# Left-over tiles of an attention and mixture-of-experts kernel: the doubling of the gathered weights placed ahead of the expert loads, and the first table tied to the last batch's split weights

## The chip, the core and the metric

The kernel runs as one program on 1 core of a Trainium2 chip. The metric is the device time of one execution in microseconds; smaller is better. TensorE is called PE below, VectorE DVE, ScalarE ACT, GpSimd POOL and SyncE SP.

## The reference, cut to what matters

```python
B, N, C, A, E, F = 4, 11456, 128, 49, 8, 1024

a2k = softmax(scale * agents @ k.T)      # 49 agents attend over the N keys
agent_v = a2k @ v                        # 49 x 128 averages in each batch
x = softmax(scale * q @ agents.T) @ agent_v   # each token mixes the 49 averages

logits = x @ w_gate
e = argmax(logits)                       # one of 8 experts for each token
gate = softmax(logits)[e]
eom = sigmoid(x @ w_output_gate)[e]
out = gate * eom * (relu(x @ w1[e]) @ w2[e])
```

Inputs and outputs are float32. All tokens of a batch mix the same 49 averages, and most of a batch's tokens choose one expert. The rest choose others; they are the left-over ("left") tokens.

## The kernel before, in words

**Main stream.** Each batch is cut into 12 units of up to 1024 tokens, and these into 92 main tiles of up to 512 tokens. For a main tile every token is computed with the expert that most of its batch chose. The averages are folded into the expert's first matrix, so a main tile multiplies the softmax weights of its tokens (`x_ld`, transposed by DMA) with `w` to give `h`; ACT writes `hh` = relu(h) in float16, DVE the remainder `hl` = relu(h) - hh, and PE then forms `y` from `hh` and `hl` with the split second matrix `vv`. The weights of a batch are split into float16 halves in `first` and `second`; the last step of `second` stores the factor `i12` in `state[b]`.

**Left tiles.** The left tokens are computed in float32 in tiles of 128, with true experts, and their results are written over the main ones by an indirect DMA. `PHASES` has two entries: the left tokens of batches 0 and 1 fill up to 12 tiles (phase 0), those of batches 2 and 3 one tile (phase 1). For each phase `left_prepare` waits until the tokens of its batches are counted (`counted[0]`, which `q_tail` sets; 3 batches for phase 0, all 4 for phase 1), builds a table in `left_table` (tiles `pexc`, `ppi`, `cnt`, `tt`, much small DVE work), and then, for groups of 3, 3, 4 and 2 tiles, runs `left_index`, which works out the token numbers `ltu` and gathers with POOL indirect DMAs the tokens' softmax weights `ef` from DRAM into the tile `big` (`bigs` in phase 1). `got` notes for each tile the planned time `t` at which its gather is in.

`left_static` runs the left tiles in two ways, every other tile in each. Its helper `fronts` prepares one tile ahead: it waits until `t`, loads the two float32 matrices of the tile's expert (`left_load`, 512 KB each, SP queue, tiles `lw_ld`), waits until both are planned to be in, and calls `left_front`. This doubles the gathered weights (one DVE product, `big<-big,ltwo`: each weight times 0 or 1 for the two batches of the phase), transposes the 128 x 98 result on PE into the bank `let`, copies it with ACT, multiplies it with the averages (`lx`) and copies that (`lxs`). `left_back` then does the two expert products (`lh`, `ly`) and `left_store` the scatter. A tile of phase 1 does its `left_back` only when the main stream is through.

**What sets the order.** Nothing is reordered by a compiler. While the program is written, a planner (`Clock`) keeps a planned time for each engine, and coroutines (`spawn`, with a priority) offer their next instruction; it is emitted when the planner has its inputs ready and the engine free. Each engine then runs its own queue strictly in the emitted order and waits on semaphores where an input is late. `big` is in `clk.apart`, so the planner doesn't look at its readiness:

```python
            clk.apart.add(big.name)
```

The transposition may thus be emitted right behind the doubling that writes its input. A POOL gather is planned with 1100 ns on POOL and 2950 ns to land, and `got` adds 2000 ns in phase 0 (none in phase 1).

Of the kernel before, what the change touches and what calls it, by code (L numbers as in the profile page):

```python
# [18 lines left out]
B, N, C, A, E, F = 4, 11456, 128, 49, 8, 1024  # L19
# [249 lines left out]
def agent_attention_top1_moe(ctx, tc, qT, kT, v, aT, wg, wo, w1, w2, cst, sides, out):  # L269
    nc = tc.nc  # L270
    clk = Clock()
    ACT, DVE, POOL = Engine(clk, "ACT", nc.scalar), Engine(clk, "DVE", nc.vector), Engine(clk, "POOL", nc.gpsimd)
# [19 lines left out]
    def n_free():  # L292
        return sum(banks[k][0] for k in others)
# [4 lines left out]
    def first_free():  # L298
        return min((when_free(banks[k]), k) for k in others if banks[k][0])

    def bank(name, dt=F32, w=512, k=None):

        k = last[0] = first_free()[1] if k is None else k
        t = ps.tile([P, w], dt, tag=f"b{k}", bufs=1, name=name)
        banks[k][1] = t.name
        return t

    def hold(long=False):

        k = last[0]  # L310
        banks[k][0] = False
        if long:
            long_held.append((k, banks[k][1]))
        return k

    def release(k):
        banks[k][0] = True
# [11 lines left out]
    def wait_free(long=False):  # L329
        while True:  # L330
            long_held[:] = [x for x in long_held if not banks[x[0]][0] and banks[x[0]][1] == x[1]]

            keep = clk.started and (long or not (Y or resting[0]))
            if n_free() > keep and not (long and len(long_held) > 1) and first_free()[0] <= clk.now() + 50.0:
                return
            yield None
# [41 lines left out]
    for i in range(4):  # L378
        t = cp.tile([P, 8, P], F16, name=f"e16_{i}")
        e16s.append(t)  # L380
    avd = []
    for i in range(2):
        t = cp.tile([P, P + 32], F32, name=f"avd_{i}")
# [3 lines left out]
    for i in range(2):  # L387
        t = cp.tile([P, 2, 18], F16, name=f"gs_{i}")
# [5 lines left out]
    for i in range(2):  # L394
        t = cp.tile([P, E, NCOL], F32, name=f"oht_{i}")
# [59 lines left out]
    state = {}  # L455
# [9 lines left out]
    def spawn(g, prio=2):  # L465
        streams.append([prio, len(streams), g, None])
        streams.sort(key=lambda x: x[0])
# [92 lines left out]
    def scored(item):  # L560
        places[held.pop(item)][0] = True
# [614 lines left out]
    counted = [0]  # L1176
# [400 lines left out]
    def left_load(ph, ti, k, nm, at_=None):  # L1577
        b0, nb, _, _ = PHASES[ph]
        yield from SY.wait(ti)
        er = nc.values_load(ti[0:1, k, 0:1], engines=[SP], min_val=0, max_val=E - 1,  # L1580
                            skip_runtime_bounds_check_because=WHY)
        if at_ is None:
            w1t = wk.tile([P, F], F32, name=f"lw1{nm}", tag="w1t", bufs=2)
        else:
            w1t = yield from at_(f"lw1{nm}")
        yield from SY.q.dma_start(w1t, w1[bass.ds(er, 1)].rearrange("a p f -> p (a f)"))
        if at_ is None:
            w2t = wk.tile([P, F], F32, name=f"lw2{nm}", tag="w2t", bufs=2)
        else:
            w2t = yield from at_(f"lw2{nm}")  # L1590
        yield from SY.q.dma_start(w2t, w2[bass.ds(er, 1)].rearrange("a p f -> p (a f)"))
        return w1t, w2t

    def left_averages(ph, nm):
        b0, nb, _, _ = PHASES[ph]
        av = wk.tile([P, C], F32, name=f"lav{nm}", tag="l_av")
        yield from SY.q.dma_start(av[0:nb * A], avnd[b0:b0 + nb].rearrange("b a c -> (b a) c"))
        return av

    def pause(ns):  # L1600

        t = clk.now() + ns
        while clk.now() < t:
            yield None

    def left_front(nm, ef, xt, two, av):
        yield from DVE.q.tensor_tensor(xt, ef[:, 0:A].unsqueeze(1).broadcast_to([P, 2, A]),
                                       two.unsqueeze(2).broadcast_to([P, 2, A]), op=ALU.mult)
        yield from wait_free()
        t = bank(f"let{nm}")  # L1610
        mark = hold()
        yield from PE.q.transpose(t[0:2 * A, 0:P], xt.rearrange("p b k -> p (b k)"), idf)
        et = wk.tile([P, P], F32, name=f"let_sb{nm}", tag="l_et")
        yield from ACT.q.copy(et[0:2 * A], t[0:2 * A, 0:P])
        release(mark)
        yield from wait_free()
        x = bank(f"lx{nm}")
        mark = hold()
        yield from PE.q.matmul(x[:, 0:P], av[0:2 * A], et[0:2 * A], start=True, stop=True)
        xs = wk.tile([P, P], F32, name=f"lxs{nm}", tag="l_xs")  # L1620
        yield from ACT.q.copy(xs, x[:, 0:P])
        release(mark)
        return xs
# [33 lines left out]
    ready, averaged = {}, {}  # L1657

    def left_prepare(ph):

        b0, nb, nst, _ = PHASES[ph]
        while counted[0] < (3 if ph == 0 else B):
            yield None
        if ph == 0:
            yield from SY.q.dma_start(ls, sides)
        yield from left_table(ph)
        averaged[ph] = yield from left_averages(ph, f"{ph}")
        i = 0
        for j, n in enumerate((3, 3, 4, 2) if nst > 2 else (nst,)):
            big = None  # L1670
            if nst > 2:
                while B - 1 not in K or K[B - 1]["s"] < min(3 * j + 3, NU):
                    yield None
                big = wk.tile([P, min(24, NCOL - 24 * j), A2], F32, name=f"big{ph}_{i}", tag=f"S{j}", bufs=1)
                big = big.rearrange("p t a -> p (t a)")

            def got(k, t, ti, tu, ef, oa, xt, two, i=i):
                ready[ph, i + k] = t, ti, k, tu[:, k:k + 1], ef[:, k, :], oa[:, k, :], xt[:, k], two[:, k, :]
            yield from left_index(ph, i, n, f"s{ph}_{i}", got, big)
            i += n  # L1680
# [9 lines left out]
    def left_static(way):  # L1690


        while way and (B - 1 not in K or K[B - 1]["v"] < NU):
            yield None
        todo = [(ph, k) for ph, x in enumerate(PHASES) for k in range(x[2])][way::WAYS]
        ops = {}
        finished = [0]

        def fronts():
            for i, (ph, k) in enumerate(todo):  # L1700
                while (ph, k) not in ready or i > finished[0]:
                    yield None
                t, ti, kk, _, ef, _, xt, two = ready[ph, k]
                yield from pause(t - clk.now())
                w1t, w2t = yield from left_load(ph, ti, kk, f"{ph}_{k}", left_place)
                yield from pause(max(clk.ready[x.name] for x in (w1t, w2t)) - clk.now())
                xs = yield from left_front(f"{ph}_{k}", ef, xt, two, averaged[ph])
                ops[ph, k] = xs, w1t, w2t

        spawn(fronts(), LEFT - 1)  # L1710
        for ph, k in todo:
            while (ph, k) not in ops:
                yield None
            xs = ops.pop((ph, k))
            while ph == len(PHASES) - 1 and not ended[0]:
                yield None
            _, _, _, tu, ef, oa, _, _ = ready[ph, k]
            yield from left_back(f"{ph}_{k}", *xs, oa, ef, ("lh", "ev")[way])
            for x in (f"lw1{ph}_{k}", f"lw2{ph}_{k}"):
                scored((x, 0, 0))  # L1720
            left.append((ph, oa, tu))
            finished[0] += 1
# [14 lines left out]
    def drain(g):  # L1737

        while True:
            try:  # L1740
                if next(g) is None:
                    clk.vt["PE"] += 100.0
            except StopIteration as stop:
                return stop.value
# [12 lines left out]
    for ph in range(len(PHASES)):  # L1757
        spawn(left_prepare(ph), 1 - ph)
# [7 lines left out]
    with tc.For_i(0, some, 1):  # L1766
        for ph, (b0, nb, nst, rows) in enumerate(PHASES):
            nr = nc.values_load(nti[ph][0:1, 0:1], min_val=0, max_val=rows,
                                skip_runtime_bounds_check_because="at most one tile per 128 tokens and one per group")
            with tc.For_i(nst, nr, 1) as i:  # L1770
                ti, tu, ef, oa, xt, two = drain(left_index(ph, i, 1, f"d{ph}"))
                w1t, w2t = drain(left_load(ph, ti, 0, f"d{ph}"))
                av = drain(left_averages(ph, f"d{ph}"))
                xs = drain(left_front(f"d{ph}", ef[:, 0, :], xt[:, 0], two[:, 0, :], av))
                drain(left_back(f"d{ph}", xs, w1t, w2t, oa[:, 0, :], ef[:, 0, :]))
                drain(left_store(ph, oa[:, 0, :], tu[:, 0:1]))

# [62 lines left out]
```

## Time and profile before

| | |
|---|---|
| median of 3 runs | 976.7 us (976.26, 976.7, 979.27) |
| profiled execution | 979.37 us, of which the profile spans 977.6 us |
| PE busy | 951.1 us (97%) |
| DVE busy | 794.2 us (81%) |
| ACT busy | 589.6 us (60%) |
| POOL busy | 348.8 us (36%) |
| left tiles' first transposition (`let`) | 768.9 us; the last one at 953.2 us |
| mean granted PE clock | 0.994 |

An engine is busy from the start to the end of its instructions; matmuls overlap, and an interval in which PE runs nothing is a wait of its queue. "Idle before, releaser" is the time that an instruction's engine had nothing to do before it, and what ended that.

### The profile page before, as it was taken

How to read it: one execution, taken by the hardware profiler on the slowest of the kernel's cores; microseconds unless marked ns; L12 is line 12 of the kernel's file. 1: busy time of each engine (PE TensorE's matmuls, PEld its weight loads, DVE VectorE, ACT ScalarE, POOL GpSimd, SP SyncE). 2: the span in 40 equal slices, each digit the busy share in tenths (PEclk: the TensorE clock that was granted, in tenths of full speed). 3: DMA queues.
4: the chain of work that ended last, by engine and by line, in shares of the span. 5: the costliest groups of instructions: out<-in, count | busy, mean ns of one | idle time of the engine just before them, and what ended most of it. 6: DMA issues, size and time to landing. Idle time of an engine off the chain costs nothing. (4 is left out here: it accounts for less than half of the span.)

```text
span 977.6 us, 37649 instructions
## 1 busy us (share of the span) xinstructions
PE 951.1 (97%) x15832; PEld 729.0 (75%) x15832; DVE 794.2 (81%) x2172; ACT 589.6 (60%) x1396; POOL 348.8 (36%) x626
## 2 busy tenths in 40 slices
PE   9999999999999999999999999999999999999996
PEld 7867777777777777777777777776767687777785
DVE  2878888889888888889888888898999887687762
ACT  2366666665756666657666666666566466555453
POOL 1013255552233364431232544522242344443221
PEclk9999999999999999999999999999999899999999
DMA  9986665546465555544567545454332444343420
GB/s 321 305 296 163 170 143 155 158 134 170 152 192 161 156 159 139 154 144 130 154 171 178 160 138 155 129 143 125 115 84 59 128 129 145 106 146 107 149 73 29
DMA packets 107997, 147.29 MB, mean 151 GB/s; under 512 B 62449, under 2 KB 70598, under 8 KB 107824
## 3 DMA queue, kind: packets, MB, share of 16 engines
q1 hardware_dynamic: 106576, 143.40, 49.9%
q8 instruction: 125, 2.05, 0.9%
q0 software_dynamic: 1248, 1.44, 0.8%
q14 instruction: 48, 0.39, 0.1%
HBM read 89.52 MB, written 35.10 MB: 127 GB/s over the span
## 5 line engine op out<-in xcount | busy, mean ns | idle before, releaser
L219 PE MATMUL y<-vv,hh 128*128 128x256 f16 (+1 forms) x2880 | 527.9, 274 | 5.0 <-DVE lL L219 2.7
L219 DVE SCALAR_TENSOR_TENSOR hl<-h,hh 128x512 f16<-128x512 f32 (+1 forms) x736 | 449.1, 668 | 95.5 <-ACT hh L219 93.1
L219 PE MATMUL y<-vv,hl 128*128 128x128 f16 (+1 forms) x2880 | 501.6, 220 | 2.6 <-DVE hl L219 1.7
L219 ACT ACTIVATE hh<-h 128x512 f16<-128x512 f32 (+1 forms) x736 | 372.0, 591 | 185.7 <-PE h L219 185.4
L219 PEld LDWEIGHTS <-hh 128*128 128x128 f16 (+1 forms) x2880 | 283.1, 98 | 57.0 <-issue 16.0
L219 PEld LDWEIGHTS <-hl 128*128 128x128 f16 (+1 forms) x2880 | 284.7, 99 | 10.2 <-DVE hl L219 5.4
L219 PE MATMUL h<-x_ld,w 128*128 128x512 f16 (+1 forms) x1472 | 256.8, 377 | 0.8 <-DVE hl L219 0.6
L219 PEld LDWEIGHTS <-w 128*128 128x128 f16 x1472 | 83.8, 95 | 110.0 <-issue 74.4
L219 POOL TENSOR_TENSOR os<-os,smt 128x512 f32<-128x512 f32 (+1 forms) x91 | 93.8, 1032 | 107.4 <-DVE os L219 59.2
L219 ACT COPY ys<-y 128x256 f32<-128x256 f32 x179 | 67.4, 377 | 103.5 <-PE y L219 102.2
L219 DVE TENSOR_TENSOR os<-y,ys 128x256 f32<-128x256 f32 x179 | 74.4, 416 | 26.9 <-ACT ys L219 25.5
L219 POOL TENSOR_TENSOR e<-ef,e 128x392 f16<-128x392 f32 (+1 forms) x48 | 43.3, 903 | 66.3 <-ACT e L219 66.1
L219 POOL TENSOR_TENSOR ev<-S,km_o 128x400 f32<-128x400 f32 (+1 forms) x36 | 32.8, 913 | 58.3 <-PE av L219 54.0
L219 POOL TENSOR_SCALAR smt<-lT,i 128x8 f32<-128x8 f32 (+1 forms) x48 | 15.8, 328 | 94.7 <-DVE lT L219 62.3
L219 PEld LDWEIGHTS ks<-at,k_ld 128*32 128x32 f32 (+1 forms) x2316 | 39.8, 116 | 10.0 <-issue 6.9
L219 PE MATMUL ks<-at,k_ld 128*32 128x50 f32 (+1 forms) x2316 | 46.4, 213 | 0.6 <-DMA k_ld<-kT 0.5
L219 PE MATMUL qs<-at,q_ld 128*32 128x50 f32 (+1 forms) x2768 | 43.0, 210 | 0.0
L219 PEld LDWEIGHTS qs<-at,q_ld 128*32 128x32 f32 (+1 forms) x2768 | 36.1, 111 | 9.0 <-issue 8.3
L219 PE MATMUL ly<-lw_ld,lh 128*128 128x128 f32 x208 | 39.1, 275 | 0.0
L219 PE MATMUL lh<-lxs,lw_ld 128*128 128x128 f32 x208 | 39.1, 275 | 0.0
L219 ACT COPY S<-ks 128x400 f32<-128x400 f32 (+1 forms) x48 | 23.6, 491 | 23.4 <-PE ks L219 23.4
L219 POOL TENSOR_TENSOR sm<-sm,ev 128x400 f32<-128x400 f32 (+1 forms) x33 | 32.2, 975 | 8.4 <-ACT ev L219 8.3
(277 smaller groups left out, 1000.0 us busy)
## 6 DMA issues: line engine op xcount, KB each, us to landing
v_ld<-v SPq DMA_DIRECT2D x44, 512.0 KB, 4.3
q_ld<-qT SPq DMA_DIRECT2D x44, 512.0 KB, 4.0
out<-os SPq DMA_DIRECT2D x88, 256.0 KB, 2.3
k_ld<-kT SPq DMA_DIRECT2D x43, 512.0 KB, 4.5
lw_ld<-w SPq DMA_DIRECT2D x26, 512.0 KB, 3.9
efd<-ef SPq DMA_DIRECT2D x44, 200.0 KB, 4.9
x_ld<-x_ld SPq DMA_DIRECT2D x132, 64.0 KB, 3.3
w1t<-w SPq DMA_DIRECT2D x4, 512.0 KB
```

The costliest lines, as they stand in the source:

```text
L219: return getattr(self.eng, op)(*a, **k)
```

## The change

The doubling becomes a generator of its own, `left_double`. In `fronts` it is emitted as soon as the planned time `t` of the gather has come, before the loads; the rest of `left_front` stays behind the loads, and also behind a planned 1000 ns after the doubling. For phase 0 `left_prepare` waits, besides the three counted batches, until `i12` of the last batch (batch 3) has been emitted. The dynamic loop at the end, for more left tiles than planned (it makes no turn with these inputs), calls the two parts one after the other.

```diff
-    def left_front(nm, ef, xt, two, av):
+    def left_double(ef, xt, two):
         yield from DVE.q.tensor_tensor(xt, ef[:, 0:A].unsqueeze(1).broadcast_to([P, 2, A]),
                                        two.unsqueeze(2).broadcast_to([P, 2, A]), op=ALU.mult)
+
+    def left_front(nm, xt, av):
         yield from wait_free()
         t = bank(f"let{nm}")
         mark = hold()
...
-        while counted[0] < (3 if ph == 0 else B):
+        while counted[0] < (3 if ph == 0 else B) or ph == 0 and "i12" not in state.get(B - 1, {}):
             yield None
         if ph == 0:
             yield from SY.q.dma_start(ls, sides)
...
                 t, ti, kk, _, ef, _, xt, two = ready[ph, k]
                 yield from pause(t - clk.now())
+                yield from left_double(ef, xt, two)
+                t = clk.vt["DVE"] + 1000.0
                 w1t, w2t = yield from left_load(ph, ti, kk, f"{ph}_{k}", left_place)
+                yield from pause(t - clk.now())
                 yield from pause(max(clk.ready[x.name] for x in (w1t, w2t)) - clk.now())
-                xs = yield from left_front(f"{ph}_{k}", ef, xt, two, averaged[ph])
+                xs = yield from left_front(f"{ph}_{k}", xt, averaged[ph])
                 ops[ph, k] = xs, w1t, w2t
```

More of the change, by code (lines that the diff above doesn't have):

```diff
@@ L1773, in agent_attention_top1_moe @@
                 av = drain(left_averages(ph, f"d{ph}"))
-                xs = drain(left_front(f"d{ph}", ef[:, 0, :], xt[:, 0], two[:, 0, :], av))
+                drain(left_double(ef[:, 0, :], xt[:, 0], two[:, 0, :]))
+                xs = drain(left_front(f"d{ph}", xt[:, 0], av))
                 drain(left_back(f"d{ph}", xs, w1t, w2t, oa[:, 0, :], ef[:, 0, :]))
```

## Prediction

> **What bounds the kernel now.** I read the page first, then PE's waits, then the view of the tile `let`, then both queues around the longest waits.
>
> ```profile
> PE 951.1 (97%) x15832; PEld 729.0 (75%) x15832; DVE 794.2 (81%) x2172; ACT 589.6 (60%) x1396; POOL 348.8 (36%) x626
> PEclk9999999999999999999999999999999899999999
> ```
>
> PE is busy for 97% of the span, so it sets the end. What a change can win is PE's idle time, or time at a lower clock (one slice shows 8 instead of 9). The stage in question begins where the left tiles come in. Busy time in the stretch before it and in it:
>
> ```profile
> core 0: us, PE busy (x) PEld busy (x) DVE busy (x) ACT busy (x) POOL busy (x), PEclk, DMA share, GB/s
> 690.00:765.00 75.00, 72.49 (x1011) 51.77 (x1010) 68.78 (x209) 45.09 (x109) 30.05 (x53) 1.00 0.34 93
> 765.00:960.00 195.00, 189.07 (x2001) 152.15 (x2000) 145.69 (x447) 110.46 (x264) 68.43 (x104) 0.98 0.38 116
> ```
>
> PE is idle for 2.5 us in the first and 5.9 us in the second. What ended its waits over 0.15 us from 765 to 960 us:
>
> ```profile
> PE let L219 <- DVE lts L219: 1.6, 2, 1.3
> PE let L219 <- issue: 1.5, 2, 1.1
> PE y L219 <- ACT big L219: 0.8, 1, 0.8
> PE let L219 <- DVE lrgs L219: 0.6, 1, 0.6
> PE let L219 <- ACT eo L219: 0.6, 1, 0.6
> PE let L219 <- PE y L219: 0.5, 1, 0.5
> PE lg L219 <- ACT big L219: 0.2, 1, 0.2
> ```
>
> The five rows of `let` make 1.6 + 1.5 + 0.6 + 0.6 + 0.5 = 4.8 us; the releasers named differ, so I looked at the queues. The longest of these waits (timeline of DVE, then PE):
>
> ```profile
> 908.56 1.88 DVE L219 SCALAR_TENSOR_TENSOR hl<-h,hh 128x512 f16<-128x512 f32 x3
> 910.42 0.17 DVE L219 COPY tot<-cum 128x8 f32<-128x8 f32 x1
> 910.50 0.26 DVE L219 TENSOR_TENSOR big<-big,ltwo_6s 128x98 f32<-128x98 f32 x1
> 910.90 0.29 PE L219 MATMUL let<-kc,big 128*98 128x128 f32 x1 [1.29 <-DVE lts L219]
> 911.79 0.29 PE L219 MATMUL pexc<-tot,kc 128*128 128x16 f32 x2
> ```
>
> and the second longest:
>
> ```profile
> 878.91 0.88 DVE L219 SCALAR_TENSOR_TENSOR leqs<-tbs,ls,leqs 16x2 f32<-16x2 f32 x1
> 879.85 0.24 DVE L219 TENSOR_TENSOR big<-big,ltwo_6s 128x98 f32<-128x98 f32 x1
> 880.19 0.29 PE L219 MATMUL let<-kc,big 128*98 128x128 f32 x1 [1.14 <-issue]
> ```
>
> Both times PE stands until the doubling ends and goes on 0.1 us later. The doubling itself takes 0.25 us; it stands in DVE's queue behind other work, and DVE runs 1 to 1.5 us behind the plan. The planner doesn't see this, since it emits the transposition right behind the doubling. So 4.8 us of PE's idle time are waits for the doubling.
>
> **The change part by part.** Nothing is removed. Added are a condition and a planned pause; moved are the 13 doublings, the 26 loads and the start of the first table.
>
> *Doubling ahead of the loads.* Between doubling and transposition now lies a tile's planned loading:
>
> ```profile
> lw_ld<-w SPq DMA_DIRECT2D x26, 512.0 KB, 3.9
> ```
>
> Two such loads one after the other; with 3.9 us from issue to landing that is more than the 1.3 us by which DVE was late at worst. The added 1000 ns lie within the loading too, so they delay nothing. The transposition finds its input ready: -4.8 us. What is late next? After 765 us PE waited for no `hl` at all (none in the list above), so DVE's lateness is covered there. Single inputs will show, though: in the rows above `pexc` would come 1.29 us earlier, at 910.5 us, while `tot` ends at 910.59, and PE would wait some 0.1 us plus the handing over. For all such returns I take 0.4 us (between 0 and 4.8, the whole gain; nearer 0, as the waits for DVE outside `let` are nil in this stage). Net -4.4 us.
>
> *Does the early doubling wait for its gather?* It would block DVE, with `hl` behind it. Each doubling waits for its own gather. It is emitted at the planned `t`, 1100 + 2950 + 2000 ns after POOL's planned issue (6.05 us; 4.05 us in phase 1). First tile and one of the long group:
>
> ```profile
> L219 DVE CAST ltu_6s<-lts x1: 170/170/170, 864.7 to 864.7; 128x4 uint32<-128x4 f32 x1
> 865.67 1.08 POOL L219 DMA_INDIRECT big<-efd,ltu_6s  x1 [1.44 <-DVE ltu_6s L219]
> DMA to landing us min/median/max: 3.0/4.1/6.5
> ```
>
> The median transfer has landed 2 us before 6.05 us are over; the slowest one is 0.8 us (POOL's start behind `ltu`) + 6.5 - 6.05 = 1.3 us late. Cost 0 to 1.3 us of DVE for each tile that starts a later group; on PE 0, since nothing waits for `hl` there. I take 0. The first group stands where DVE is full (this view holds its gathers and that of phase 1):
>
> ```profile
> DMA to landing us min/median/max: 2.3/3.7/5.1
> ```
>
> With the same 0.8 us and 5.1 us at most, it is 5.9 us against 6.05: 0 as well. For phase 1 it is 5.9 against 4.05, up to 1.9 us of DVE, again where PE waits for no `hl`: 0.
>
> *Loads behind the doubling's slot.* SP's two loads are emitted only when the planner has found DVE free, up to one block of four `hl` later (2.48 us in the timeline). Before, the same slot was waited for after the loads, so a tile's chain is as long as it was. Queued behind these loads on SP are the transfers of `x_ld`, `out` and `q`; they come earlier relative to the loads, if anything. Cost 0.
>
> *First table behind `i12`.* In the trace (DVE, and the PE row of the tile):
>
> ```profile
> 673.23 0.79 DVE L219 COPY tot<-cum 128x8 f32<-128x8 f32 x1
> 679.03 0.15 DVE L219 TENSOR_TENSOR i<-s_si 128x1 f32<-128x1 f32 x1
> 679.44 0.16 DVE L219 TENSOR_TENSOR ppi<-pexc,tot 128x16 f32<-128x16 f32 x1
> 680.04 2.48 DVE L219 SCALAR_TENSOR_TENSOR hl<-h,hh 128x512 f16<-128x512 f32 x4
> L219 PE MATMUL pexc<-tot,kc x2: 263/273/283, 675.3 to 675.4; 128*128 128x16 f32 x2
> ```
>
> The table's first DVE step already stood just behind `i12`. Only `pexc` moves, behind `i12`, and `ppi` then probably falls behind the next four `hl`: about 3 us later (between 0.4 and 5.8 + 2.5 = 8.3 us, the whole distance from `tot` to `i12` and a block). The left tiles are filling work and end long before the main stream:
>
> ```profile
> 938.17 1.95 SPq L219 DMA_DIRECT2D lw_ld<-w  x2
> 943.05 1.04 POOL L219 DMA_INDIRECT bigs<-efd,ltu_0s  x1 [2.16 <-issue]
> L219 PE MATMUL let<-kc,bigs x1: 273/273/273, 953.2 to 953.2; 128*98 128x128 f32 x1
> 955.92 0.39 PE L219 MATMUL lx<-let_sb,lav 98*128 98x128 f32 x2
> 964.56 2.00 PE L219 MATMUL lh<-lxs,lw_ld 128*128 128x128 f32 x16
> ```
>
> Only the tile of phase 1 must come after the main stream (from 964.56 us); its `lx` is done at 956.3 us, 8 us earlier. With PE 4.4 us faster some 3.8 us are left. Cost 0.
>
> *A new order of everything after 679 us.* The planner places all later work anew. What it can win or lose is the rest of PE's idle time, 2.5 + 5.9 - 4.8 = 3.6 us: from -3.6 (all gone) to +3.6 us (doubled). Nothing speaks for a side; I take 0.
>
> *The clock.* One stretch of the profiled execution ran at half clock:
>
> ```profile
> 768.10:771.50 3.40, 3.26 (x28) 1.89 (x28) 3.40 (x8) 2.53 (x6) 0.29 (x1) 1.00 0.25 72
> 771.50:778.30 6.80, 6.05 (x31) 3.60 (x31) 5.14 (x19) 3.67 (x10) 2.95 (x5) 0.50 0.10 39
> ```
>
> 6.8 us at half clock cost PE 3.4 us. In the 3.4 us before it lie the first `let` and the narrow products of an index group, with PE's loads busy for just over half. The timed runs lie at 976.26, 976.7 and 979.27 us, the profiled one at 979.37: two groups 2.6 to 3.1 us apart, about what this stretch costs. My estimate is that the median ran without it.
>
> The Trainium skill, TensorE: Matmul & The Clock Gate, section "What's actually happening", says that the activity is judged in windows of about 3.4 us that run freely, not from the kernel's start. The length of the stretch, two such windows, agrees; by that rule the stretch would come in some executions of one and the same program, which is the first rival below.
>
> **The sum.** Against the profiled execution: 979.37 (span 977.6 and 1.8 us around it) - 4.8 + 0.4 = 975.0 us with the stretch, and 971.6 us without. Against the median, which I take to be without: 976.7 - 4.4 = **972.3 us**.
>
> One rule speaks against the change. A small DVE step can take far longer while POOL works (tile `lfs`):
>
> ```profile
> L219 DVE TENSOR_SCALAR lfs<-lccs x5: 148/162/885, 749.6 to 941.2; 128x3 f32<-128x3 f32 x2, 128x4 f32<-128x4 f32 x1, 128x2 f32<-128x2 f32 x1, 128x1 f32<-128x1 f32 x1
> 749.57 0.90 POOL L219 TENSOR_TENSOR e<-ef,e 128x392 f16<-128x392 f32 x1 [2.81 <-ACT e L219]
> ```
>
> The longest fell on a POOL product at 749.6 us. The Trainium skill, GPSIMD Engine Reference, section "Key points", says that POOL shares its SBUF interfaces with DVE, and that DVE instructions with two SBUF inputs contend; the doubling has two and moves towards POOL's gathers. At 0.885 - 0.162 = 0.7 us each that is DVE time after 765 us, where PE doesn't wait for it, and 0.7 us of PE at the first tile at most: by that rule 973.0 us, by the row of the doubling itself (0.25 us each time) 972.3.
>
> **The rivals.**
> - *The half-clock stretch stays, in most runs.* For it: the index groups keep their narrow products, and the first `let` stays near the second group. Against: by these times it came in two of four executions, and at one of four index groups, and PE now waits less. 972.3 + 3.4 = 975.7 us, within 0.3%.
> - *The waits come back elsewhere.* DVE stays as late as it is, and PE meets it at `pexc`, at the index products or at `y`; or DVE is so late that even a tile's loading doesn't cover it. For it: the `pexc` row above. Against: no wait for `hl` after 765 us. With 0 to 1 us left of the gain: 976.2 us.
> - *The new order also drops the other waits*, most of 3.6 us, for instance those for `hl` before 765 us: 968.7 us.
> - *Slower: the last tile comes late.* Place: `lx` and `lh` of the phase 1 tile at the end. If the first table moves by d and the ways pass that on, PE idles for d - 3.8 us before the last `lh`; an idle of 3.4 us can also halve the clock for the tile's last 4 us of products, 4 us more. It decides from d = 7.2 us on; at the upper bound, 8.3 us: 972.3 + 4.5 + 4.0 = 980.8 us. Against: `ppi` stood behind `i12` already, and this tile has a table of its own.
>
> **How the numbers follow.** 0.3% of 976.7 us is 2.9 us, about what a measurement can tell from no change: faster is below 973.8, slower above 979.6. Chances: the forecast 0.46 (its own range 970.5 to 973.7), stretch stays 0.17, waits come back 0.15, other waits go too 0.12, last tile late 0.10. Faster 0.46 + 0.12 = 0.58, same 0.17 + 0.15 = 0.32, slower 0.10. The range goes from 968.5 (the fourth case, just held) to 977.5 (the second and third with an us of new order); it leaves out the late tile and some of the edges.
>
> **What would show it.** Right: PE's waits have no `let` row from 765 us on, or under 0.5 us in all; each doubling ends some us before its transposition; PE's idle time there falls from 5.9 to about 1.5 us. A doubling that waits for its gather shows as DVE idle just before `big<-big,ltwo`. The first table's `ppi` is to stand 0.4 to 8 us after `i12`, and the last `lh` right behind the last `y`. I am wrong if PE's waits for `hl`, `tot` or ACT grow by what `let` loses, if a second half-clock stretch appears before the end, or if PE idles before the last `lh`.

## Result and profile after

The changed kernel took 971.3 us (median of 5 runs, 970.68 to 972.19), beside 977.8 us (976.26 to 979.27, 5 runs) for the kernel before on the same chip: ratio 0.9936, 95% interval 0.9921 to 0.995. In later runs beside other kernels it took 971.31 us against 977.17 us (0.9946, 0.9929 to 0.9962). The forecast was 972.3 us.

The profiled execution after took 970.68 us (span 968.9). From its page, PE's busy time and the clock of the 40 slices:

```profile
PE 947.1 (98%) x15832; PEld 727.5 (75%) x15832; DVE 797.1 (82%) x2172; ACT 588.4 (61%) x1396; POOL 348.3 (36%) x626
PEclk9999999999999999999999999999999999999999
```

The slower slice is gone. PE's idle time fell from 977.6 - 951.1 = 26.5 us to 968.9 - 947.1 = 21.8 us: 4.7 us. Its busy time fell by 4.0 us; about 3.0 of them are the half-clock stretch of the execution before, in which PE was busy for 6.05 us, half of it lost. The same two stretches of time as before the change:

```profile
core 0: us, PE busy (x) PEld busy (x) DVE busy (x) ACT busy (x) POOL busy (x), PEclk, DMA share, GB/s
690.00:765.00 75.00, 72.68 (x1008) 51.74 (x1007) 70.86 (x212) 43.83 (x108) 30.66 (x55) 1.00 0.32 82
765.00:960.00 195.00, 193.78 (x2085) 158.87 (x2082) 148.16 (x452) 111.90 (x270) 69.07 (x105) 1.00 0.39 122
```

From 690 to 765 us PE idles 2.3 us (2.5 before), from 765 to 960 us 1.2 us (5.9 before). All 4.7 us thus come from the stage with the left tiles. What ended PE's waits there (view of waits, 765 to 960 us: total, times, longest):

```profile
PE y L219 <- ACT lh L219: 0.7, 1, 0.7
PE lh L219 <- ACT lxs L219: 0.2, 1, 0.2
```

The five rows of `let` are gone. In the timeline, one doubling and one transposition for each of two tiles, the second being phase 1's:

```profile
919.69 0.25 DVE L219 TENSOR_TENSOR big<-big,ltwo_10s 128x98 f32<-128x98 f32 x1
924.60 0.27 PE L219 MATMUL let<-kc,big 128*98 128x128 f32 x1
...
946.68 0.25 DVE L219 TENSOR_TENSOR bigs<-bigs,ltwo_0s 128x98 f32<-128x98 f32 x1
951.93 0.27 PE L219 MATMUL let<-kc,bigs 128*98 128x128 f32 x1
```

From the end of the doubling to the transposition it is 4.7 and 5.0 us, where before it was 0.1 us at eleven of the thirteen tiles. The doubling itself still takes 0.25 us here.

The start of the first table (timeline, DVE and PE):

```profile
678.50 0.15 DVE L219 TENSOR_TENSOR i<-s_si 128x1 f32<-128x1 f32 x1
678.63 0.29 PE L219 MATMUL pexc<-tot,kc 128*128 128x16 f32 x2
679.02 0.12 DVE L219 TENSOR_TENSOR ppi<-pexc,tot 128x16 f32<-128x16 f32 x1
679.24 2.48 DVE L219 SCALAR_TENSOR_TENSOR hl<-h,hh 128x512 f16<-128x512 f32 x4
681.97 0.15 DVE L219 COPY cnt<-cnt 128x8 f32<-128x8 f32 x1
```

`pexc` moved behind `i12` (tile `i`) as forecast, but `ppi` stands 0.5 us after `i12` and still ahead of the block of four `hl`; before, it stood 0.4 us after. And at the end of the program:

```profile
955.89 0.22 PE L219 MATMUL y<-vv,hl 128*96 128x128 f16 x1
955.95 2.00 PE L219 MATMUL lh<-lxs,lw_ld 128*128 128x128 f32 x16
```

The last tile's `lh` follows the last `y` without a gap.

### The profile page after: what moved, and what is told of

Read it like the earlier page. It is cut to its first block, busy times and chain, and to the rows that moved or that the text cites. A ratio compares the mean times of both kernels' runs of the same rounds, so it can differ in the third digit from the quotient of the medians.

```text
span 968.9 us, 37640 instructions
## 1 busy us (share of the span) xinstructions
PE 947.1 (98%) x15832; PEld 727.5 (75%) x15832; DVE 797.1 (82%) x2172; ACT 588.4 (61%) x1396; POOL 348.3 (36%) x626
## 5 line engine op out<-in xcount | busy, mean ns | idle before, releaser
L219 PEld LDWEIGHTS <-x_ld 128*128 128x128 f16 x360 | 27.0, 98 | 12.0 <-issue 5.9
```

The costliest lines, as they stand in the source:

```text
L219: return getattr(self.eng, op)(*a, **k)
```

## Experiments

Theory A: the gain is PE's waits for a doubling that ended too late, and what takes them away is distance in PE's queue between doubling and transposition. Theory B: it is the later start of the first table. Theory C: it is any new order of the work after 679 us.

**e1_early_only and e2_gate_only: one part each.** e1 is the changed kernel without the condition on `i12`; e2 is the kernel before with that condition alone.

```diff
 # e1, against the changed kernel
-        while counted[0] < (3 if ph == 0 else B) or ph == 0 and "i12" not in state.get(B - 1, {}):
+        while counted[0] < (3 if ph == 0 else B):
 # e2, against the kernel before: the same line the other way round
```

> The doubling is moved ahead of the loads, the first table starts as before (no wait for i12). Theory A (PE's waits for a late doubling are the gain): PE's waits at let vanish (4.8 us before), 971 to 973 us. Rival B (the gain comes from the table behind i12 and the new order that follows from it): 975 to 978 us, let waits or others of the same size remain. Rival C (half or more of the gain is the half-clock stretch, which goes with whatever order comes out): let waits vanish, but the time is 974 to 976 us where a half-clock stretch before the end stays.

> Only the first table waits for i12 of the last batch; doubling as before. Theory A: PE still waits about 4 to 5 us at let, 976 to 978.5 us, within 0.3% of before. Rival B: 971 to 973.5 us. Rival C: the clock stretch decides, 973.5 to 975 us without one in any run, 977 to 979 with one.

e1: 971.39 us (ratio to before 0.9936, 0.9919 to 0.9954). PE's waits from 765 to 955 us:

```profile
PE y L219 <- DVE qz L219: 0.7, 1, 0.7
PE tbs L219 <- DVE big L219: 0.5, 1, 0.5
PE cnt L219 <- DVE ppi L219: 0.2, 1, 0.2
PE lg L219 <- ACT let_sb L219: 0.2, 1, 0.2
```

e2: 976.95 us against 977.2 us (0.9996, 0.9984 to 1.0008), with these rows of `let`:

```profile
PE let L219 <- DVE big L219: 2.2, 3, 1.6
PE let L219 <- issue: 1.3, 2, 1.2
```

The doubling's move alone makes the whole gain, and the condition alone none that can be measured. Theory B falls. e2 also has a new order after 679 us and gains nothing from it, which speaks against theory C.

**e3_hold_only, e8_hold_500, e10_hold_200, e11_hold_0: distance without the early place.** The doubling stays behind the loads, and the planner holds the transposition until 1000, 500, 200 or 0 ns after the doubling's planned end on DVE. The first table begins as before.

```diff
 # e3, against the changed kernel without the condition on i12
                 yield from pause(t - clk.now())
-                yield from left_double(ef, xt, two)
-                t = clk.vt["DVE"] + 1000.0
                 w1t, w2t = yield from left_load(ph, ti, kk, f"{ph}_{k}", left_place)
-                yield from pause(t - clk.now())
                 yield from pause(max(clk.ready[x.name] for x in (w1t, w2t)) - clk.now())
+                yield from left_double(ef, xt, two)
+                yield from pause(clk.vt["DVE"] + 1000.0 - clk.now())   # e8: 500.0, e10: 200.0, e11: + nothing
```

> The doubling stays behind the loads, but the planner holds the transposition a planned 1000 ns behind it; no wait for i12. Theory A (what counts is the distance between doubling and transposition, and DVE is late by up to 1.3 us): of the waits 1.29, 1.14, 0.76, 0.63, 0.56 and smaller ones only what exceeds about 1 us stays, under 0.8 us at let in all; 971.5 to 974 us. Rival D (the early place itself counts, since 1000 ns don't cover DVE's lateness): 2 us or more of let waits, 974.5 to 977 us.

> The doubling stays behind the loads and a planned hold of 500 ns (1000 ns in e3) stands between it and its transposition; the first table begins as before. Theory A (PE waits for a doubling that DVE does late, and only the distance in the plan counts): the waits of `let` before were about 1.3, 0.3, 1.1, 0.4, 0.6, 0.6 and 0.5 us; less 0.5 us each they leave 0.8 + 0.6 + 0.1 + 0.1 = 1.6 us, so 977.2 - 3.2 = 974.0 us (973 to 975), with `let` rows of 1 to 2.2 us in PE's waits. Rival (any new order after 679 us is worth the 6 us, whatever the distance): no `let` rows, about 971.5 us, as in e3. Rival (the distance must cover DVE's whole lateness or it gives nothing): 976.5 us or more.

> As e8, with a planned hold of 200 ns between doubling and transposition. With 500 ns the distance from the doubling's end to the transposition was 0.07 to 2.2 us in the trace and about 0.54 us smaller at the last seven tiles than with 1000 ns. Theory A (distance): 0.3 us less again, so that some six of the thirteen transpositions stand right at the doubling's end, with 0.8 to 2 us of `let` waits in PE's list: 972 to 974 us. Rival (any hold above nothing lets the planner put other products ahead, and that is all it takes): `let` waits under 0.5 us, 971.5 us. Rival (the order alone): no relation to the hold, anything from 971 to 977 us with `let` rows absent.

> The hold between doubling and transposition is only up to the doubling's own planned end on DVE (0 ns more). The planner leaves the tile `big` out of its look at what is ready, so in the kernel before it could place the transposition while its own plan had DVE still at or ahead of the doubling: counted in its plan, DVE's planned time lay up to 0.45 us ahead of PE's at the transpositions. Theory A1 (most of the 4.8 us stood in the plan itself and was not seen for that reason): this hold alone takes most of it away, `let` waits of 0.5 to 2 us in all, 971.5 to 973.5 us. Theory A2 (DVE on the chip runs 1 to 1.5 us behind its plan, as the prediction says): a hold of nothing leaves the lateness, `let` waits of 3 us or more, 975 us or more.

| kernel | median us | ratio to before (95%) | `let` waits, 765 to 955 us |
|---|---|---|---|
| e3, 1000 ns | 971.53 | 0.9947 (0.9929 to 0.9965) | none |
| e8, 500 ns | 971.47 | 0.9948 (0.9931 to 0.9965) | 0.3 + 0.2 us |
| e10, 200 ns | 971.72 | 0.9947 (0.9927 to 0.9967) | 0.4 + 0.3 us |
| e11, 0 ns | 972.71 | 0.9948 (0.9932 to 0.9964) | 0.4 + 0.3 us |

The rows of e11:

```profile
PE let L219 <- ACT hh L219: 0.4, 1, 0.4
PE let L219 <- PE y L219: 0.3, 1, 0.3
```

Two things follow. The early place isn't needed: a hold behind the loads gives the same time. And the size I expected from the hold was wrong: I had the waits shrink by the hold's length, to 1.6 us at 500 ns. Already a hold that ends with the doubling's planned end leaves only 0.7 us. The line `clk.apart.add(big.name)` keeps the planner from looking whether `big` is ready, so waits could stand in the plan itself. By the planner's own times, written out while the program is built, the transposition of the kernel before starts ahead of the doubling's planned end at nine of the thirteen tiles, by 0.07 to 0.45 us, 2.4 us in all; in e11's plan it does so at none. With the 0.1 us from each doubling's end to its transposition this makes some 3.3 of the 4.8 us, by this estimate. Told of that time, the planner puts other products first. In e8, DVE and then PE (the dots stand for products `ly` and `y`):

```profile
907.82 0.26 DVE L219 TENSOR_TENSOR big<-big,ltwo_6s 128x98 f32<-128x98 f32 x1
908.06 0.39 PE L219 MATMUL ly<-lw_ld,lh 128*128 128x128 f32 x2
...
908.84 0.27 PE L219 MATMUL let<-kc,big 128*98 128x128 f32 x1
```

PE works through `ly` and `y` while DVE doubles, and comes to the transposition 0.8 us after the doubling has ended.

DVE was late on the chip at the two longest waits of before (1.29 and 1.14 us). Ahead of the longest, its small step `lmis` took 1.16 us, where the median of the five such steps is 0.16, and DVE then worked with hardly a pause up to the doubling. POOL ran a product `os` in that time (DVE, then POOL):

```profile
906.22 1.16 DVE L219 TENSOR_SCALAR lmis<-lmis 128x2 int32<-128x2 int32 x1
906.21 1.03 POOL L219 TENSOR_TENSOR os<-os,smt 128x512 f32<-128x512 f32 x1 [1.91 <-DVE lmis L219]
```

Ahead of the second longest it is `leqs`, 0.88 us where the median is 0.20 (878.91 us in the prediction's rows), beside a POOL product `os` from 878.74 to 879.78 us. The two steps took 1.0 and 0.7 us more than usual. In e11 both remaining waits of `let` also come behind such a step. At the shorter it is `lr`, 1.06 us from 831.27 us, beside a product `os` from 830.84 to 832.26 us; the longer one (DVE, POOL, DVE, PE):

```profile
792.90 0.97 DVE L219 SCALAR_TENSOR_TENSOR a<-se,d 128x8 f32<-128x8 f32 x1
792.82 1.03 POOL L219 TENSOR_TENSOR os<-os,smt 128x512 f32<-128x512 f32 x1 [1.44 <-DVE os L219]
793.80 0.25 DVE L219 TENSOR_TENSOR big<-big,ltwo_0s 128x98 f32<-128x98 f32 x1
794.15 0.29 PE L219 MATMUL let<-kc,big 128*98 128x128 f32 x1 [0.40 <-ACT hh L219]
```

Each of these long steps ends within 0.15 us of POOL's product. That the product holds DVE up is read from these rows; no run here takes it away.

In the changed kernel itself the added `pause(t - clk.now())` changes nothing: without it the planner writes the same instructions in the same order.

**e4_doubled_twice: the early place, without the distance.** The changed kernel, with the same doubling done a second time right ahead of the transposition. DVE has 13 more doublings of 0.25 us.

```diff
                 yield from pause(max(clk.ready[x.name] for x in (w1t, w2t)) - clk.now())
+                yield from left_double(ef, xt, two)
                 xs = yield from left_front(f"{ph}_{k}", xt, averaged[ph])
```

> The changed kernel, with the same doubling done a second time where it was before, right ahead of the transposition (it writes the same values again). 13 more DVE products of 0.25 us each, 3.2 us of DVE off PE's path. Theory A: PE waits at let again, 3 to 5 us, 974 to 977 us. Rival B (order and table are the gain): 971 to 972.5 us, as the changed kernel.

976.11 us (ratio 0.9987, 0.9977 to 0.9996), with waits from 765 to 955 us of

```profile
PE let L219 <- DVE big L219: 1.4, 3, 0.6
PE let L219 <- ACT hh L219: 0.7, 1, 0.7
PE let L219 <- DVE t1i L219: 0.5, 1, 0.5
PE let L219 <- DVE a L219: 0.4, 1, 0.4
```

3.0 us of `let` waits are back, and with them most of the 6 us. Some 0.7 us of them come from one of the added doublings, which itself took 1.04 us (rows in the last section). e3 and e4 together show that the distance counts, in either place of the doubling. Theory C falls: e1, e3, e8, e10 and e11 differ in order and agree within 1.3 us; e2 and e4 have new orders and stay near the kernel before.

**e7_banks_later (with after_again beside it), e14_margin_before, e15_margin_250, e12_hold_500_margin: the same idea elsewhere.** The planner begins filling work in a bank of PSUM up to 50 ns ahead of the bank's planned release. e7 makes that 500 ns behind it:

```diff
-            if n_free() > keep and ... and first_free()[0] <= clk.now() + 50.0:
+            if n_free() > keep and ... and first_free()[0] <= clk.now() + (-500.0 if clk.started else 50.0):
```

(e7 has a second condition, on the bank of `y`; without it PE's order comes out the same.) e14 is the kernel before with this edit, e15 the changed kernel with 250 ns, e12 is e8 with 500 ns; after_again is the changed kernel itself.

> The changed kernel, in which the planner also starts filling work and `y` in a bank of PSUM only when the bank has been planned free for some time (500 ns and 700 ns), so that PE finds the bank drained. Theory A carried on (an engine in order that runs behind its plan should be kept at a distance from its reader): of the changed kernel's idle time of PE, 21.8 us, the waits for banks, some 3 us, go: about 968.5 us. Rival (the bank waits are PE running ahead of its plan and come back at another product, or the distance leaves the filling work too late): 971 us or slower, up to 980 us if the left tiles come late.

> The changed kernel itself, beside these two on the same chip. Theory A: 971.3 us (970.5 to 972.5), no wait of `let`, and no run far above the others if the stretch at half clock stays away; if that stretch comes and goes by itself, one run in three stands about 1.7 us higher.

> The kernel before, where filling work starts in a bank of PSUM only when the bank has been planned free for 500 ns (before: up to 50 ns ahead of its planned release). This edit alone makes the order of e7, 968.5 us, out of the changed kernel's. If the margin's gain (2.8 us: PE's waits at `lg` go, 1.7 us, and some of the time from an `h` to an `lg`) and the doubling's add up: 977.2 - 2.8 = 974.4 us, with the `let` rows still there (3 to 5 us). Rival (the margin also puts distance ahead of the transposition, since it waits for a bank between doubling and transposition): `let` rows under 1.5 us and 970 to 972 us. Rival (e7 is a lucky order): 977 us or slower.

> The changed kernel with half of e7's margin: filling work starts in a bank planned free for 250 ns. If the margin is what counts: between 968.5 and 971.3 us, with `lg` waits under 0.8 us. If e7 is a lucky order: 971.3 us or above, waits of `lg` as in the changed kernel (1.7 us).

> e8 (hold of 500 ns, doubling behind the loads, first table as before) with the margin of e7 and e14 (filling work starts in a bank planned free for 500 ns). If both add up as e14 showed: 971.5 - 2.6 = 968.9 us (968 to 970), no `let` waits over 0.5 us, no `lg` waits. If the doubling ahead of the loads matters once the other waits are gone: 970.5 us or more, above e7's 968.5.

e7 took 968.46 us (968.15 to 971.62, 4 runs), against 971.31 us for the changed kernel beside it and 977.17 us before: ratio to before 0.9922, 0.9901 to 0.9942. Its median is the lowest of these kernels, but its interval overlaps the changed kernel's (0.9929 to 0.9962). Two groups of the changed kernel (busy us, mean ns, idle time before them and what ended it):

```profile
L219 PE MATMUL y<-vv,hh 128*128 128x256 f16 (+1 forms) x2880 | 526.6, 273 | 5.0 <-DVE lL L219 2.3 <-ACT ys L219 0.9 <-ACT lh L219 0.7
...
L219 PE MATMUL lg<-gs,x_ld 128*128 128x36 f16 x360 | 33.3, 180 | 1.7 <-DVE os L219 0.6 <-DMA x_ld<-x_ld 0.5 <-DVE qz L219 0.4
```

The same groups in e7, and the busy times of its page (span 966.4 us):

```profile
L219 PE MATMUL y<-vv,hh 128*128 128x256 f16 (+1 forms) x2880 | 528.1, 273 | 8.7 <-DVE lL L219 3.4 <-DVE s_s L219 1.9 <-ACT S L219 1.8
...
L219 PE MATMUL lg<-gs,x_ld 128*128 128x36 f16 x360 | 33.3, 179 | 0.0
```

```profile
PE 943.3 (98%) x15800; PEld 725.3 (75%) x15800; DVE 798.6 (83%) x2172; ACT 589.7 (61%) x1396; POOL 349.5 (36%) x626
```

The waits at `lg` went, but those of this `y` rose from 5.0 to 8.7 us (for `lL` from 2.3 to 3.4 us), and PE's idle time in all from 21.8 to 966.4 - 943.3 = 23.1 us. The gain shows as less busy time of PE, 943.3 against 947.1 us; which products got cheaper the trace doesn't say clearly (the records are also 32 fewer). So the expected mechanism, waits for banks, is not what gave the time.

e14 gave 974.57 us against 976.91 (0.9983, 0.997 to 0.9996), near the 974.4 expected, with 2.1 us of `let` waits left. e15 gave 970.94 us (0.9931, 0.9911 to 0.9952): its `lg` waits are down to 0.5 us, but its median is only 0.4 us below the changed kernel's, which these runs can't tell from nothing. e12 gave 972.01 us (0.9947, 0.9931 to 0.9963), where 968.9 was expected, with no `lg` waits and 0.5 us of `let` waits. By the medians the margin is thus worth 2.3 us on one order, 2.8 on another and nothing on a third, though the `lg` waits are 0 on each. Whether e7 owes its time to the margin or to an order that happens to suit it isn't settled, nor whether the doubling ahead of the loads is what e12 lacks.

## Why the prediction was right, and where it wasn't

- **Doubling ahead of the loads.** Right in size: 4.8 us of `let` waits went, and PE's idle time fell by 4.7 us, where -4.4 was taken. The return of 0.4 us did not come at `pexc`, which has no wait; instead `y` waits 0.7 us for `lh`, which about takes the place of the 0.8 us of `y` for `big` before.
- **Why those waits were there** is the step that failed: "DVE runs 1 to 1.5 us behind the plan" and "The planner doesn't see this, since it emits the transposition right behind the doubling". By e11 most of the waits go when the planner merely respects its own plan of DVE; the blind spot is the tile `big`, left out of its look at readiness. In that plan 2.4 us of the waits stood already. DVE was late on the chip at the two longest waits, by about 1.0 and 0.7 us, each time behind a small step that took that much longer beside a POOL product. For the time this made no difference, since a tile's loading covers either. For the lesson it does: a much smaller edit than the change gives about its gain.
- **The gather and the loads, both taken at 0.** No DVE idle time stands before a doubling in the trace after, and no wait for a load among PE's rows above. Right.
- **First table behind `i12`.** "about 3 us later" was too much: `ppi` kept its place ahead of the four `hl`, 0.5 us after `i12`. By e2 the whole condition (976.95 against 977.2 us) can't be told from nothing. The fear of a late last tile fell with it.
- **A new order**, 0 with ±3.6 us: e1, e3, e8 and the changed kernel lie within 0.3 us of each other.
- **The clock.** The middle one of the three runs shown, 976.7 us, agrees with the runs without the half-clock stretch; the stretch's cost was put too high: PE was busy for 6.05 of the 6.80 us, so at half clock it lost about 3.0 us, not 3.4. Of 52 later runs of the kernel before, 24 had a mean granted clock of 0.996 or less, with a median of 978.26 us; the other 28 have 976.66 us. That is 1.6 us: mostly one stretch of half the length, since 17 of the 24 have a mean clock of 0.995, as has e4's profile, which holds such a one:

```profile
768.06:771.46 3.40, 3.27 (x28) 1.88 (x26) 3.36 (x9) 2.68 (x6) 0.30 (x1) 1.00 0.80 291
771.46:774.87 3.41, 3.41 (x16) 1.86 (x15) 3.41 (x14) 1.38 (x5) 2.03 (x3) 0.50 0.21 78
```

  3.41 us at half clock cost 1.7 us. The changed kernel had a clock that low in 1 of 9 runs. Comparing only runs above 0.996, the change is worth 976.66 - 971.17 = 5.5 us (the latter the median of 8 runs): 4.7 us of idle time, and 0.8 us that I can't place. It lies in PE's busy time, which fell by 4.0 us in the profiled executions, about 1.0 more than the stretch accounts for.
- **The rule on the shared SBUF interface** (the Trainium skill, GPSIMD Engine Reference, "Key points"), by which the time would have been 973.0 us: in the trace after the doublings take 0.20 to 0.25 us, so the forecast without it held. The partner that was feared, POOL's indirect DMAs, lengthens none of them: the doubling at 946.68 us ran its 0.25 us wholly beside one. POOL's product `os` does so in other runs: doublings took 1.04 us in e4, 0.76 and 0.96 us in e2, 0.60 and 1.10 us in e14. That is 0.35 to 0.85 us more than usual, where 0.7 us was put. In the trace after, no doubling starts while such a product runs.
- **The rivals.** Waits elsewhere did not come back, the other waits did not go (1.2 us are left, as forecast about 1.5), and the last tile was not late. The half-clock stretch, judged by that mean clock, did not stay "in most runs": 1 in 9; in the other kernels with little or no waiting at `let` it came in 13 of 38, so the change does not rule it out.

## What to carry to other kernels

Where a planner writes each engine's order, look for tiles whose readiness it does not track: an in-order engine then stands at the reader, and the profile can name something else as the releaser than the late writer. Read the timeline of both queues around the longest waits, and test the remedy by distance alone, with the least hold first, before moving work. Where the writer is late, look for a step ahead of it that took far longer than its fellows, and at what POOL did then. And where one edit in the order pays, repeat it on another order before calling it a rule: by the medians the margin paid 2.3 and 2.8 us on two orders and nothing on a third.

## What was unexpected of the hardware

A stretch at half clock comes in the middle of a busy kernel, in some executions of one and the same program and not in others: 24 of 52, judged by the mean clock. It comes at different places too: in e1's profile PE's clock halves from 823.8 us on, for twice 3.4 us:

```profile
820.40:823.80 3.40, 2.72 (x18) 1.33 (x16) 3.37 (x10) 2.57 (x6) 0.40 (x1) 1.00 0.31 98
823.80:830.60 6.80, 6.80 (x37) 5.57 (x37) 5.01 (x15) 2.03 (x5) 1.61 (x3) 0.50 0.21 39
```

In the 3.4 us ahead of these stretches PE was busy for 2.72 and 3.27 us, with few products (18 and 28) and its loads busy for only 1.33 and 1.88 us. The lengths agree with the windows of about 3.4 us that run freely (the Trainium skill, TensorE: Matmul & The Clock Gate, "What's actually happening"); what tips a window was not tested.

A DVE step of 0.15 to 0.25 us can take about 1 us when it starts while POOL runs a product `os`. In the rows shown it ends with that product, or up to 0.15 us later. In e4 this struck a doubling (DVE, POOL, PE):

```profile
903.09 1.04 DVE L219 TENSOR_TENSOR big<-big,ltwo_6s 128x98 f32<-128x98 f32 x1
902.94 1.07 POOL L219 TENSOR_TENSOR os<-os,smt 128x512 f32<-128x512 f32 x1 [0.59 <-DVE lmis L219]
904.22 0.29 PE L219 MATMUL let<-kc,big 128*98 128x128 f32 x1 [0.66 <-ACT hh L219]
```

It isn't always the doubling that is struck: in e15 one began 0.1 us after such a product and took 0.24 us, and the step behind it took 0.99 us. That POOL's product is the cause is read from the times; no run tested it.
